# Pair 14 attended row by row, one-column scale and bias, more warm-up matmuls, and a re-sorted instruction order in an attention and gating kernel

## The chip, the cores and the metric

The kernel runs on one core of a Trainium2 chip, as one program with one launch. The metric is device time in microseconds (us), the median of several runs. The profile is one further execution of the same program, with its own time.

## The reference

Clustered attention comes first. Queries and keys are each assigned to the nearest of 16 centroids of their head. A query sees only the keys of its own cluster. Then a gated MLP mixes the tokens.

```
q_assign = argmax(q_n @ c_n^T);  k_assign = argmax(k_n @ c_n^T)      # (4, 8, 768), 16 clusters
scores   = where(q_assign == k_assign, q @ k^T / 8, -1e9)            # (4, 8, 768, 768)
attn     = exp(scores - max) / (sum + 1e-9);  x = attn @ v           # x: (4, 768, 512)
h = relu(x @ w_in);  u, v = split(h)                                 # w_in: 512 x 1024
v_s = w_spatial @ layernorm(v) + b_spatial;  out = (u * v_s) @ w_out # w_spatial: 768 x 768
```

## The kernel before

Four batches with eight heads each are worked as 16 pairs of heads, numbered 0 to 15, four to a batch. Pair n is prepared (prep), its shift is found (shifts), and it is attended (attend). After the four pairs of batch b, its MLP follows (mlp): six tiles each of V, U, S and O work. All products are taken in float16 parts, high and low, so most matmuls come in twos or threes.

There are two ways to attend a head. In the usual way, a first pass of matmuls (shifts, L1011) computes the scores of a head only for their row maxima, which VectorE reduces (L1018). The negated maxima go as three extra columns through a transposing DMA (sht<-shx, L1060) and a small DMA (hq<-sht, L1061) into the operands. The second pass (L1179, L1181) then has keys as rows, ScalarE takes exp with constant scale and bias (L1186), casts the result to its high part (L1201), GpSimd subtracts for the low part (L1202), and the value matmuls follow (L1208). A mean of the values enters for queries without keys, by small matmuls (L776, and L1208 from mean) and two DMAs.

In the other way (turned, for the heads listed in TURNED: both heads of pairs 11, 13 and 15) the scores are computed once, with queries as rows (L1086, L1088), two row tiles at a time. VectorE reduces the maxima (L1096, L1105) and makes a scale sl (L1106) and a bias bi (L1107) of two columns each, one column per row tile. ScalarE takes exp with them (L1115) and casts (L1125), GpSimd subtracts (L1126), and a transposing DMA of 128 x 1536 float16 per row tile (L1127, from one of three buffers to one of three others, named pt or wraw) brings the probabilities into the form that the value matmuls (L1134 to L1136) take.

Everything is first put down as operations with their dependences, and then a planner (Plan.run) issues them in the order of a simulated time. Among the operations that are ready on an engine it takes the one with the smallest due number. These numbers stand in a packed table (STARTS), one for each operation. Each engine runs its own list in that fixed order, and waits where an operand is not there. The planner's costs (DMA, LATE_PAD, PE_PAD and others) shape this order and nothing else. The eight PSUM banks are eight tiles named acc. A first group of matmuls of constants (keep_warm, L644) holds one of them from its first matmul to its last. These matmuls stand behind everything else in priority, and WARM lists the earliest planned time of each: 50, at 2.0 to 16.7 us. Five more stand ahead of the last O tile. SP's queue issues nearly all DMAs, in order, and ScalarE's queue the output.

Of the kernel before, what the change touches and what calls it, by code (L numbers as in the profile page):

```python
# [17 lines left out]
P = 128  # L18
# [51 lines left out]
LATE_PAD = 0.8  # L70
PE_PAD = 0.15
DMA = {
    "raw": (3.12, 0.57, 1.01, 0.36),
    "raw0": (1.26, 0.64, 1.0, 0.44),
    "vraw": (1.46, 0.43, 0.82, 0.36),
    "hqhq": (2.23, 0.77, 0.43, 0.68),
    "half": (0.25, 0.34, 0.88, 0.5),
    "lo": (0.95, 0.18, 1.02, 0.52),
    "mean": (0.0, 0.53, 0.43, 0.62),
    "row": (0.45, 0.7, 1.11, 0.61),  # L80
    "sht": (0.0, 0.51, 0.65, 0.73),
    "ohx": (1.39, 0.37, 0.53, 1.25),
    "shx": (0.9, 1.12, 0.53, 1.25),
    "xhl": (1.58, 1.01, 0.74, 1.4),
    "pt": (1.58, 1.01, 0.74, 1.4),
    "ghl": (1.55, 0.53, 0.67, 1.25),
    "out": (0.96, 0.07, 0.32, 0.34),
    "win": (1.77, 1.35, 0.88, 0.6),
    "wou": (1.12, 1.38, 0.9, 0.6),
    "wsp": (0.92, 0.17, 0.77, 0.55),  # L90
# [99 lines left out]
    "knv<9nL=ifg=9{dR~D7|WK~&LR+p`0Cpk~9mV4wOd0Nhp>*P*(RGyRf<VX2el8Ud=sVu6Ls;=s)daAx^rrM}Ns<P^-7O0b|f$F73s@ZC}+Nyr4OuC`2rK{_fx|8m&hw4#!w4S0T>IOPOPt*JKVSQbFP#g47eL|np"  # L190
    "H}qT0OqfY-Qkm?gj45s^nEa-&DP_{>uKJX&ZyK34rnd<<gUvki&^$G9>`1#wAJd7<Ff-XqF{{mPbHp^Xk#?e8XgAm=I>_8Lugp91*`%`L?G!uNZnAsqVVeqam_nwlnPV23WoCzYXTREDNCO$57*vDNW~^CfHkk|N"
    "qOmp;WQ5|-6k0<ESniIR)8>wGHm*%#Prx;J3U8pN>+80<W_}spF7NOM{1N}imx@_3R2-9uM0$}+lobO+FVRQL5og6Uaao)Zzh#heN~+8%wW^@XshBdMOe|B$Br>_oB-6-rGONribI5|Sk}NLE$U3r`oG;hPm2#2X"
    "CZEe%vbL-t8_CA9oopjJ%FeR4>?ViGVRDchDaXsPa<UZ4D^#H>r>d!n$?~$CtSqa@da{A6FZ;?4GD1#}O=Jt%P<EG1Wqa9E4wR8{rko_V$ksAS_LHMz4>?B8k;~+HIah9$C*^DTOumvz1=KjXSWcB|<TSZZu9v&y"
    "Q+Yt1kniPwc|`7(m*qiuTwahDC0Cc^U71*2mAB<X`9(gEPvjf<QYKK}B~$5DQB_QpRaI4O6;oFdRn%}XS&R`=M1NUA?H7a9IdMfi7GDIHz2smyTrQQH<VLwcwpIhx1$9H+Rd3WQ^;{j6XXP1rMc$B)<Slt!ev;qh"
    "2l+=nmM`Ql8AHWWAu5yVq&ll^YJi%q{z;>fs|+fY%A?|_FqK2)Qw3CEl|~g&rB!oPO*K_R)h%^X-B$ON(r@Kg`B_>8Dp+ZiQZ-g-RaVtq#Z`$^LX|=#RT))YRYUbw*;GL_Naa$+Rc_TtWmgqdOVvS5RDD%{HC3%r"
    "$J9AhLf6q<R7cfbjZke>A2m#kS1Z&QHAQVxqtrMxTFq0_)GReaEmgbK617&HQghWJwNPzT%hYPMR~=O^)E;$6y;bdWd)-0L(yR0#eM@A}D3i+QGOoNSzpDZ=w=OAb%9gT^94)WOJMx{3u41ZaDwZm(`)JUwRVw{M"
    "<<y0BE!9pnR6W!XH9<wFu_{sxS98>QHA$^hGu0ZkT^(0m$I&Tt8l6qI((BYFwMCs!m(>|{N!?S2)iw1@S*^9xOh?x-bTr*X&(#a{Y`s=r(7V(TwND*TJJo6RM7>w2FRH65uD+sPs)y>cdZa!oq5r5b{Z|F)jQWd`"
    "`nL+zTpJy%W9xD{sZOb@>P32^-l?DI=Q^Mh=;S)Jj-_+x%({^7tc&XkI$USb1$9wfNmtPobz|L3Pu6X8Z#`94)-`lJT~pW9t#uDQP%qIV^(4Js2OBU+%r~9Uj4`d$Rg+(pQI%8+l}Fb$O;k?PRrOPg)n>IpomXeo"
    "9ra6nQ=imVb;H~?C(Lnk(ws5Z%yo0c#M23Ne4SVq(D`*fol6(dC3P8HRyWs8bbZ}cx6nQHS#6Cop(d%xW4h^Hx~cB2`|1&ToSv^E^>`hn=jrKso1Uqc>eYIW_GXe9Z=%cuGvD;n!}TCNSP#%+^a{OPpVwRUUj0DN"
    "(9851eME28+x0<xT>sNo^=17<AJEtINqtLS*LU?({YI1dsDJ5%rnD(yN|@<pmU*S`>xcS-exzUPzgn2ICd9-t1<hw2*L>HpO>`6Aq%j#xK9kv`Fm=pVoy>5P#TZk?G%&?XN7K~QFg?s7v&1YgTg-N|-<&m<%mee)"  # L200
    "aC_6-GSAHy^Iy)`zlPb&Hml8Iv)TN%q^)4f+G;kB&1Xy5Wp=f#ZR^;kcCB4yx7p=(tKDID+P!v*Jz}re7xuUPY|q&n_My!JS>e6aAR!-=fa*{mnm{{f2rXa)jD?xd8-~CX_+|fD1B+oN><8t*g}ThHwQu7)_&q)^"
# [12 lines left out]
    "-4*x9-EuG7YxmBPfA7AyARmIUFgm8d<oLurbI;v3_tJfEpWQE)$^UiEXZK&-Z^ymy-<|crK87#iWBRzhtXJOq=swhk_(VRN&*{ti{JxNH>9b*O%!j401lGs<@Yg>B>D~glYVN9!=^pwlF0D)Na=N@OpDW;sxW=xk"
    "tL&P(7?=zh0xEPE4dY^b%;4TZHuoKJxo=R{rFH{dDL2ejax+~+H^+5!<6H+9+b8u&e3<X#pZG~`nw#ZjxQTAITkKZ3b#9B><c_!l?w~v5F1r)%tV{04`zSxzON@<id^8`+$Mf-hLZ8N`^of0HpV7DQZGC6I)u;Cv"
# [243 lines left out]
def kernel(  # L459
# [130 lines left out]
    def idt():  # L590
        return scratch.t[:, 0, 2 * D:2 * D + P]
# [853 lines left out]
```

## Time and profile before

| what | us |
|---|---|
| median of three runs | 651.34 (649.42 to 653.78) |
| profiled execution, its own time | 650.55 |
| its span, first to last instruction | 648.7 |
| TensorE (PE) busy, VectorE (DVE) busy | 626.9, 421.4 |
| ScalarE (ACT) busy, GpSimd (POOL) busy | 462.4, 443.3 |

A busy PE is not PE at its peak, since matmuls overlap and their ends are modelled. PEclk is the granted clock of TensorE: 1.00 is 2.4 GHz and 0.50 is 1.2 GHz. An idle engine matters only where the work that it delays ends last.

### The profile page before, as it was taken

The page shows a single profiled execution, that of the slowest core. Times are in us where ns is not written, and L with a number is a line of the kernel's source. Part 1 is how long each engine was busy: PE and PEld are TensorE (multiplying, and loading weights), DVE is VectorE, ACT ScalarE, POOL GpSimd, SP SyncE. Part 2 cuts the span into 40 slices and gives each one's busy share as a digit, 9 for nine tenths or more (in the row PEclk, how much of TensorE's full clock was granted, in tenths as well). Part 3 has the DMA queues.
Part 4 walks back from the last instruction along what each step waited for, and adds up shares of the span by engine and source line. Part 5 has one row for each costly group of instructions (what it writes and reads, how often), then busy time and mean ns, then how long its engine had stood idle before and what let it go on. Part 6 is the DMA issues. An engine that isn't in the chain of part 4 may idle for free.

```text
span 648.7 us, 16743 instructions
## 1 busy us (share of the span) xinstructions
PE 626.9 (97%) x6696; PEld 379.0 (58%) x6696; DVE 421.4 (65%) x795; ACT 462.4 (71%) x881; POOL 443.3 (68%) x376
## 2 busy tenths in 40 slices
PE   8889999999999999999999989999899999999997
PEld 3456777766676665466665645665556555444443
DVE  5969999999998996649667786754730961132000
ACT  5778899999999996268875878685778774242221
POOL 3476789899999997069984864786689775152210
PEclk9888999999999999999999999999899999999999
DMA  6575797979737588414636197964784479512223
GB/s 191 147 143 125 160 209 135 194 168 171 187 81 171 101 175 201 104 63 116 146 98 138 32 183 147 182 120 80 155 155 73 91 148 187 90 33 50 49 65 97
DMA packets 157975, 83.67 MB, mean 129 GB/s; under 512 B 142113, under 2 KB 145226, under 8 KB 157898
## 3 DMA queue, kind: packets, MB, share of 16 engines
q1 hardware_dynamic: 154154, 75.92, 58.4%
q10 hardware_dynamic: 3744, 6.69, 3.0%
q8 instruction: 52, 0.85, 0.6%
q14 instruction: 25, 0.20, 0.1%
HBM read 27.66 MB, written 6.29 MB: 52 GB/s over the span
## 4 chain that ended last, share of the span: by engine, by line
PE 68%; ACT 11%; DVE 9%; DMA 4%; issue 4%; POOL 4%; POOLq 0%; SPq 0%; ACTq 0%; DVEq 0%
PE acc L1280 33%; PE acc L1208 10%; PE acc L1181 6%; PE acc L1179 6%; PE acc L1011 5%; ACT p L1186 3%; ACT p L1115 2%; DVE nm L1018 2%; PE acc L644 2%; DVE nm L1096 2%; ACT pt L1201 2%; POOL pt L1202 2%; DMA gT<-ghl 1%; DMA sht<-shx 1%; DMA hq<-sht 1%
## 5 line engine op out<-in xcount | busy, mean ns | idle before, releaser
L1202 POOL TENSOR_TENSOR pt<-p,pt 128x768 f16<-128x768 f32 x148 | 252.0, 1723 | 35.6 <-ACT pt L1201 24.9
L1018 DVE TENSOR_REDUCE nm<-acc 128x1 f32<-128x512 f32 (+1 forms) x234 | 150.3, 680 | 24.2 <-PE acc L1011 21.4
L1186 ACT ACTIVATE p<-acc 128x512 f32<-128x512 f32 x234 | 129.0, 604 | 21.7 <-PE acc L1181 14.1
L1280 PE MATMUL acc<-win,xT 128*128 128x512 f16 x576 | 133.7, 379 | 0.2 <-ACT p L1115 0.2
L1201 ACT CAST pt<-p 128x768 f16<-128x768 f32 x148 | 120.2, 844 | 13.7 <-PE acc L1208 7.4
L1208 PEld LDWEIGHTS <-pt 128*128 128x128 f16 x2664 | 96.5, 97 | 20.2 <-POOL pt L1202 3.2
L1208 PE MATMUL acc<-vhl,pt 128*128 128x65 f16 x2664 | 103.5, 193 | 2.2 <-POOL pt L1202 2.1
L1280 PE MATMUL acc<-vn,wsp 128*128 128x512 f16 x432 | 101.4, 379 | 0.3 <-ACT p L1115 0.3
L1181 PE MATMUL acc<-hq 81*128 81x512 f16 (+1 forms) x312 | 91.7, 335 | 2.9 <-DMA hq<-sht 2.1
L1179 PE MATMUL acc<-hq,lo 128*128 128x512 f16 (+1 forms) x312 | 91.2, 333 | 0.4 <-ACT p L1186 0.2
L1280 PEld LDWEIGHTS <-xT 128*128 128x128 f16 x576 | 54.7, 98 | 60.6 <-issue 0.5
L1011 PE MATMUL acc<-hq 80*128 80x256 f16 (+1 forms) x312 | 78.6, 331 | 1.4 <-ACT p L1186 0.5
L1126 POOL TENSOR_TENSOR pt<-p,pt 128x768 f16<-128x768 f32 x36 | 59.0, 1644 | 26.1 <-ACT pt L1125 19.5
L1352 POOL TENSOR_TENSOR ghl<-u,ghl 128x512 f16<-128x512 f32 x24 | 28.5, 1189 | 64.8 <-ACT ghl L1351 64.8
L1280 PE MATMUL acc<-wou,gT 128*128 128x512 f16 x288 | 67.6, 379 | 0.6 <-DMA gT<-ghl 0.6
L1280 PEld LDWEIGHTS <-wsp 128*128 128x128 f16 x432 | 41.1, 98 | 45.6 <-issue 0.4
L1350 DVE SCALAR_TENSOR_TENSOR u<-acc,bsp,u 128x512 f32<-128x512 f32 x24 | 18.0, 748 | 75.6 <-PE acc L1280 73.6
L1115 ACT ACTIVATE p<-acc,bi,sl 128x512 f32<-128x512 f32 (+1 forms) x72 | 42.9, 676 | 14.2 <-DVE bi L1107 12.3
L1280 PEld LDWEIGHTS <-gT 128*128 128x128 f16 x288 | 27.5, 98 | 32.2 <-DMA gT<-ghl 1.3
L1179 PEld LDWEIGHTS <-lo 128*128 128x128 f16 x312 | 30.0, 99 | 26.8 <-issue 5.5
L1096 DVE TENSOR_REDUCE nm<-acc 128x1 f32<-128x512 f32 (+1 forms) x54 | 34.8, 680 | 11.2 <-PE acc L1088 11.1
L1011 PEld LDWEIGHTS <-hq 80*128 80x128 f16 x312 | 28.4, 100 | 20.0 <-issue 4.2
(154 smaller groups left out, 989.4 us busy)
## 6 DMA issues: line engine op xcount, KB each, us to landing
raw<-in_kqT_dram SPq DMA_DIRECT2D x15, 768.0 KB
vraw<-in_vp_dram SPq DMA_DIRECT2D x16, 384.0 KB
out_dram<-o ACTq DMA_DIRECT2D x24, 256.0 KB
hq<-hq SPq DMA_DIRECT2D x15, 384.0 KB
vn<-in_w_in_dram SPq DMA_DIRECT2D x8, 512.0 KB
hq<-lo SPq DMA_DIRECT2D x15, 192.0 KB
lo<-hq SPq DMA_DIRECT2D x15, 192.0 KB
wraw<-in_wsT_dram SPq DMA_DIRECT2D x12, 192.0 KB
```

What stands on the lines that cost most here:

```text
L1011: T.matmul(out=acc.t[:, c:c + cs.stop - cs.start], lhsT=hq.t[0:R_SH, 1, h, t * P:(t + 1) * P], rhs=hq.t[0:R_SH, 0, h, cs], start=c == 0, s ...
L1018: V.tensor_reduce(out=nm.t[:, t, k:k + 1] if n == 1 else nm.t[:, t:t + n, k], in_=src, axis=AX.X, op=ALU.max, negate=True)
L1096: V.tensor_reduce(out=nm.t[:, t, k:k + 1] if n_ == 1 else nm.t[:, t:t + n_, k], in_=src, axis=AX.X, op=ALU.max, negate=True)
L1115: A.activation(out=p32.t[:, j, halves[x]], in_=sc.t[:, j * (S - 512):(j + 1) * (S - 512)] if x else sc.t, func=AF.Exp, bias=bi.t[:, t:t + ...
L1126: c = op("POOL", 1.64, lambda pt=pt, j=j, p32=p32: G_.tensor_tensor(out=pt.t[:, S:], in0=p32.t[:, j, :], in1=pt.t[:, 0:S], op=ALU.subtract ...
L1179: T.matmul(out=o, lhsT=lo.t[:, h, ks], rhs=hq.t[:, 2, h, cs], start=x == 0, stop=False, skip_group_check=True)
L1181: T.matmul(out=o, lhsT=hq.t[0:R_E, 0, h, ks], rhs=hq.t[0:R_E, 1, h, cs], start=False, stop=True, skip_group_check=True)
L1186: o = op("ACT", 0.6, lambda: A.activation(out=p32.t[:, j0:j0 + n_, cs], in_=sc.t.rearrange("p (t c) -> p t c", t=n_), func=AF.Exp, bias=P_ ...
L1201: o = op("DVE" if fast else "ACT", C_CAST if fast else 0.83, lambda pt=pt, p32t=p32t, fast=fast: (V.tensor_copy if fast else A.copy)(out=p ...
L1202: o = op("POOL", 1.64, lambda pt=pt, p32t=p32t: G_.tensor_tensor(out=pt.t[:, S:], in0=p32t(), in1=pt.t[:, 0:S], op=ALU.subtract), after=[o ...
L1208: T.matmul(out=a[:, c * W:c * W + w], lhsT=lhsT, rhs=rhs, skip_group_check=True, **f)
L1280: T.matmul(out=acc.t[:, 0:w], lhsT=lr[m][0], rhs=lr[m][1], start=(m == 0), stop=(m == n - 1))
```

## The change

Both heads of pair 14 join TURNED. For the pairs in TS1 (11, 13 and 14) scale and bias are made one column at a time: four small operations for two row tiles in place of two, the bias by a tensor_scalar with the scale as its second operand, and each exp waits only for its own column. Pair 15 keeps the two-column form. WARM grows from 50 to 145 matmuls, the last at 45.2 us. The planner's DMA costs and pads change, it now reckons with instruction fetches that block the DMA rings (FETCH), and the table STARTS is another one, so the order on every engine is sorted anew.

```diff
-LATE_PAD = 0.8
-PE_PAD = 0.15
+LATE_PAD = 0.4
+FETCH = (128, 256, 2.6, 0.95)
+PE_PAD = 0.1
...
-    "pt": (1.58, 1.01, 0.74, 1.4),
+    "pt": (1.85, 1.01, 0.25, 1.42),
...
-TURNED = ((11, 0), (11, 1), (13, 0), (13, 1), (15, 0), (15, 1))
+TURNED = ((11, 0), (11, 1), (13, 0), (13, 1), (14, 0), (14, 1), (15, 0), (15, 1))
+TS1 = (11, 13, 14)
...
+                    count += 2 * o.mms
+                    while count >= nxt:
+                        fetch.append(s + FETCH[2])
+                        nxt += FETCH[1]
...
+            if n in TS1:
+                ys = []
+                for t in range(t0, t0 + 2):
+                    y = op("DVE", 0.1, lambda t=t: V.tensor_scalar(out=sl.t[:, t:t + 1], in0=nl.t[:, t:t + 1], scalar1=LIM, scalar2=SC_UNIT, op0=ALU.is_lt, op1=ALU.mult), after=[o], ...)
+                    ys.append(op("DVE", 0.1, lambda t=t: V.tensor_scalar(out=bi.t[:, t:t + 1], in0=nl.t[:, t:t + 1], scalar1=P_LOG * LN2 / SC_UNIT, scalar2=sl.t[:, t:t + 1], op0=ALU.add, op1=ALU.mult), after=[y], ...))
+            else:
+                (the two operations of before, with both columns)
+                ys = [o, o]
...
-                    e = op("ACT", (0.6, 0.4)[x], ex, after=[o], ...)
+                    e = op("ACT", (0.6, 0.4)[x], ex, after=[ys[j]], ...)
```

## Rows read from the trace of the kernel before

**Rows 1.** Busy time of each engine (instructions), then PEclk, DMA share, GB/s, by stretch
```profile
80.00:100.00 20.00, 19.63 (x291) 15.07 (x288) 18.71 (x35) 19.88 (x41) 17.91 (x13) 1.00 1.00 210
180.00:200.00 20.00, 20.00 (x317) 14.30 (x314) 19.12 (x33) 19.97 (x41) 19.76 (x15) 1.00 0.52 128
```
**Rows 2.** The chain that ended last: start us, us, what
```profile
553.87 75.12 PE acc L1280 x348
```
**Rows 3.** Columns as in the first group: stretches with a lowered clock
```profile
30.00:35.00 5.00, 5.00 (x50) 2.81 (x49) 2.48 (x6) 5.00 (x13) 4.61 (x3) 0.51 0.66 150
45.00:50.00 5.00, 4.00 (x13) 1.87 (x13) 1.57 (x3) 2.32 (x6) 2.13 (x2) 0.52 0.54 133
50.00:55.00 5.00, 5.00 (x62) 3.23 (x61) 4.31 (x7) 4.20 (x9) 3.28 (x3) 0.80 1.04 228
...
460.00:465.00 5.00, 4.40 (x45) 3.00 (x45) 4.46 (x11) 5.00 (x9) 2.64 (x2) 0.66 0.43 82
```
**Rows 4.** The chain that ended last, around 46 us: start us, us, what
```profile
42.99 2.97 DMA hq<-sht
...
48.72 0.43 PE acc L1179
```
**Rows 5.** Columns as in the first group: the room for them
```profile
20.00:40.00 20.00, 17.18 (x204) 10.86 (x202) 17.01 (x34) 14.68 (x37) 10.85 (x8) 0.83 0.68 166
40.00:60.00 20.00, 17.35 (x203) 11.64 (x203) 15.45 (x30) 13.41 (x25) 14.00 (x10) 0.83 0.59 123
```
**Rows 6.** VectorE in order of time: start us, us, instruction
```profile
5.66 0.15 DVE L620 TENSOR_SCALAR ninv<-nrm 128x1 f32<-128x1 f32 x1 [0.67 <-POOL nrm L618]
...
457.68 1.49 DVE L1107 SCALAR_TENSOR_TENSOR bi<-nl,sl 128x2 f32<-128x2 f32 x1
...
511.85 1.56 DVE L1106 TENSOR_SCALAR sl<-nl 128x2 f32<-128x2 f32 x1
...
517.28 0.17 DVE L1106 TENSOR_SCALAR sl<-nl 128x2 f32<-128x2 f32 x1
```
**Rows 7.** GpSimd in order of time, the same stretches
```profile
457.51 1.64 POOL L1126 TENSOR_TENSOR pt<-p,pt 128x768 f16<-128x768 f32 x1
...
511.74 3.24 POOL L1126 TENSOR_TENSOR pt<-p,pt 128x768 f16<-128x768 f32 x2 [0.18 <-ACT pt L1125]
```
**Rows 8.** Costliest groups: busy us, mean ns of one, then idle before
```profile
L1107 DVE SCALAR_TENSOR_TENSOR bi<-nl,sl 128x2 f32<-128x2 f32 x18 | 12.1, 671 | 0.4
```
**Rows 9.** TensorE in order of time: start us, us, instruction, idle before and its releaser
```profile
460.03 0.38 PE L1086 MATMUL acc<-lo,hq 128*128 128x512 f16 x1 [1.28 <-ACT p L1115]
```
**Rows 10.** Groups of instructions by form: the pass for maxima and the mean, 13 pairs
```profile
L1011 PE MATMUL acc<-hq 80*128 80x512 f16 x156 | 55.8, 384 | 1.0 <-DVE nm L1018 0.4 <-DVE hq L860 0.2 <-ACT p L1186 0.2
L1011 PE MATMUL acc<-hq 80*128 80x256 f16 x156 | 30.7, 279 | 0.4 <-ACT p L1186 0.3
...
L1208 PE MATMUL acc<-mean,hq 83*128 83x65 f16 x156 | 9.0, 193 | 1.1 <-DMA hq<-sht 1.1
```
**Rows 11.** Columns as in the first group: pairs 13, 14 and 15 in turn
```profile
440.00:480.00 40.00, 38.15 (x349) 21.59 (x347) 21.31 (x51) 27.75 (x48) 28.82 (x34) 0.96 0.71 136
480.00:505.00 25.00, 24.14 (x297) 15.21 (x296) 4.18 (x12) 21.71 (x40) 22.34 (x16) 1.00 0.49 88
505.00:550.00 45.00, 42.70 (x455) 24.66 (x454) 25.60 (x45) 29.85 (x49) 30.89 (x22) 1.00 0.78 139
```
**Rows 12.** DMA from 464 to 495 us: queue, packets, MB, share of 16 engines; then issues
```profile
q1 hardware_dynamic: 14664, 3.67, 73.9%
...
pt<-pt SPq DMA_TRANSPOSE x5
wraw<-pt SPq DMA_TRANSPOSE x3
gT<-ghl SPq DMA_TRANSPOSE x2
```
**Rows 13.** The chain that ended last, in pair 14: start us, us, what
```profile
486.88 5.44 DMA pt<-pt
```

More of the change, by code (lines that the diff above doesn't have):

```diff
@@ L284 @@
 class Op:
-    __slots__ = ("eng", "cost", "fn", "after", "order", "new", "claim", "key", "at", "dma", "turn", "cols", "due", "left", "ready", "outs", "end", "seq", "alt", "s", "free", "port", "tag", "gen", "post", "issue")
+    __slots__ = ("eng", "cost", "fn", "after", "order", "new", "claim", "key", "at", "dma", "turn", "cols", "due", "left", "ready", "outs", "end", "seq", "alt", "s", "free", "port", "tag", "gen", "post", "issue", "mms")
 LAG = {"PE": 0.2, "ACT": 0.034, "DVE": 0.034, "POOL": 0.034, "SP": 0.0, "NONE": 0.0}
@@ L317, in ring, with op @@
         return r
-    def op(self, eng, cost, fn, after=(), use=(), new=(), claim=(), key=0.0, at=0.0, dma=None, turn=False, cols=0, alt=None, due=None, port=None):
+    def op(self, eng, cost, fn, after=(), use=(), new=(), claim=(), key=0.0, at=0.0, dma=None, turn=False, cols=0, alt=None, due=None, port=None, mms=0):
         o = Op()
+        o.mms = mms
         o.due = self.due if due is None else due
@@ L361, in run @@
         hw = [0.0, FIRST]
+        count, nxt, fetch = 0, FETCH[0], []
         lanes = []
@@ L443, in run @@
                 hw[0] = h + o.gen
-                d = max(h + o.gen + 0.65, hw[1])
-                hw[1] = d + o.dma
-                o.end = d + o.dma + o.post
+                more = 0.0
+                while True:
+                    d = max(h + o.gen + 0.65, hw[1])
+                    x = d + o.dma + more
+                    if not fetch or fetch[0] >= x:
+                        break
+                    f = fetch.pop(0)
+                    if f > d:
+                        more += FETCH[3]
+                    else:
+                        hw[1] = max(hw[1], f) + FETCH[3]
+                hw[1] = x
+                o.end = x + o.post
                 lanes.append(o.end)
-                free[e] = max(s + o.issue, d + o.dma - 0.9 if o.turn else h)
+                free[e] = max(s + o.issue, x - o.turn if o.turn else h)
             o.s, o.free = s, free[e]
@@ L627 @@
     ct = r_acc.new()
-    o = op("PE", 0.3, lambda: T.transpose(out=ct.t[:, 0:P], in_=scratch.t[:, 0, 0:2 * D], identity=idt()), after=[o, ld_i], use=[scratch], new=[ct], key=KC)
+    o = op("PE", 0.3, lambda: T.transpose(out=ct.t[:, 0:P], in_=scratch.t[:, 0, 0:2 * D], identity=idt()), after=[o, ld_i], use=[scratch], new=[ct], key=KC, mms=1)
     c_cm = []
@@ L644, in run @@
                 T.matmul(out=tok.t, lhsT=ones, rhs=ones.unsqueeze(1).broadcast_to([P, 4, P]), start=True, stop=True)
-            o = op("PE", 0.2145, run, after=after, at=at, use=[tok] if k else [], new=[] if k else [tok], cols=512, key=FILLER + k)
+            o = op("PE", 0.2145, run, after=after, at=at, use=[tok] if k else [], new=[] if k else [tok], cols=512, key=FILLER + k, mms=1)
     if WARM:
@@ L1011, in scores @@
                         T.matmul(out=acc.t[:, c:c + cs.stop - cs.start], lhsT=hq.t[0:R_SH, 1, h, t * P:(t + 1) * P], rhs=hq.t[0:R_SH, 0, h, cs], start=c == 0, stop=c > 0 or n == 1, skip_group_check=True)
[L1013 removed]
+                o = op("PE", 0.2185, scores, after=ready(parts) + maxed[-MX_AHEAD:][:1], use=[hq], new=[acc], cols=512, key=K0_MX + K0_HEAD * h if n_ == 0 else K_MX, mms=n)
                 def most():
@@ L1088, in scores @@
                                 T.matmul(out=o, lhsT=hq.t[0:R_SH, 1, h, ts], rhs=hq.t[0:R_SH, 0, h, cs], start=False, stop=True, skip_group_check=True)
-                o = last["sc"] = op("PE", 0.436, scores, after=X["go"][h] + [last.get("sc")] + exps[-SQ_AHEAD:][:1], use=[hq, lo], new=[sc], cols=1024, key=K_SC)
+                o = last["sc"] = op("PE", 0.436, scores, after=X["go"][h] + [last.get("sc")] + exps[-SQ_AHEAD:][:1], use=[hq, lo], new=[sc], cols=1024, key=K_SC, mms=2 * len(spans))
                 new = not tops and t0 == 0
@@ L1117, in turned @@
                     new = not got and j == 0
-                    e = op("ACT", (0.6, 0.4)[x], ex, after=[o], use=[sc, sl, bi] + ([] if new else [p32]), new=[p32] if new else [], key=K_EXP)
+                    e = op("ACT", (0.6, 0.4)[x], ex, after=[ys[j]], use=[sc, sl, bi] + ([] if new else [p32]), new=[p32] if new else [], key=K_EXP)
                     exps.append(e)
@@ L1136, in values @@
                         T.matmul(out=o, lhsT=l, rhs=vh.t[:, k, h, 0:D + 1], start=False, stop=k == NT - 1, skip_group_check=True)
-                prev = op("PE", 0.545, values, after=[c, prev] + X["v"] + (xread.get(b - 2, []) if t == 0 else []), use=[tp, vh] + ([av] if t else []), new=[] if t else [av], cols=18 * 65, key=AV_KEY)
+                prev = op("PE", 0.545, values, after=[c, prev] + X["v"] + (xread.get(b - 2, []) if t == 0 else []), use=[tp, vh] + ([av] if t else []), new=[] if t else [av], cols=18 * 65, key=AV_KEY, mms=3 * NT)
                 plan.tag = "s%d%d" % (n, 2 * h + t0 // 3)
@@ L1181, in scores @@
                                     T.matmul(out=o, lhsT=hq.t[0:R_E, 0, h, ks], rhs=hq.t[0:R_E, 1, h, cs], start=False, stop=True, skip_group_check=True)
-                    o = last["sc"] = op("PE", 0.436, scores, after=X["go"][h] + [X["shift"][h][0 if len(X["shift"][h]) == 1 else spans[0][1].start // 512], last.get("sc")] + exps[-SC_AHEAD:][:1], use=[hq, lo], new=[sc], cols=1024, key=K_SC)
+                    o = last["sc"] = op("PE", 0.436, scores, after=X["go"][h] + [X["shift"][h][0 if len(X["shift"][h]) == 1 else spans[0][1].start // 512], last.get("sc")] + exps[-SC_AHEAD:][:1], use=[hq, lo], new=[sc], cols=1024, key=K_SC, mms=2 * len(spans))
                     j0, cs = spans[0][0] % 2, spans[0][1]
@@ L1226, in attend @@
                 plan.tag = "a%d%d" % (n, 2 * h + k // 3)
-                prev = op("PE", (C_F32 if whole else 0.516 if two else 0.545) + (0.175 if k == 0 else 0), values, after=got + [prev] + X["v"] + (xread.get(b - 2, []) if k == 0 else []), use=[pt, X["vf"] if whole else vh, mw] + (avs if k else [hq]), new=[] if k else avs, cols=18 * 65, key=AV_KEY)
+                prev = op("PE", (C_F32 if whole else 0.516 if two else 0.545) + (0.175 if k == 0 else 0), values, after=got + [prev] + X["v"] + (xread.get(b - 2, []) if k == 0 else []), use=[pt, X["vf"] if whole else vh, mw] + (avs if k else [hq]), new=[] if k else avs, cols=18 * 65, key=AV_KEY, mms=NT * ((1 if whole else 2 if two else 3) + (k == 0)))
                 if whole:
```

153 lines of the change are left out of this document (78 added, 75 removed).

## The prediction

> **What bounds the kernel now.** I read the busy time of each engine in stretches of 20 us first, because the stages have different limits. Up to 140 us only attention runs, and ScalarE and VectorE are full: 19.88 and 18.71 of 20 us [rows 1]. From about 180 us the MLP of an earlier batch fills every gap of TensorE, which is busy 20.00 of 20 [rows 1], and the end is TensorE alone: 348 MLP matmuls in 75.12 us, 0.216 us each [rows 2]. So the time is TensorE's work plus the time in which it stands or runs at half clock, wherever that is. Two places have such time. The first is 20 to 60 us, where TensorE is busy 17.18 and 17.35 of 20 us at a mean clock of 0.83 [rows 5]. The second is the last batch of attention, 440 to 550 us: 38.15 of 40, 24.14 of 25 and 42.70 of 45 us busy, 5.0 us idle in all [rows 11]. An early microsecond saved is saved at the end too, since what follows is bound by full engines first and by TensorE's list of work later.
>
> **Matmuls of constants.** The granted clock is 0.51 in 30 to 35 us, 0.52 in 45 to 50 and 0.80 in 50 to 55 [rows 3]; it is the lower level, 1.2 GHz, most of that time. It falls after TensorE stood waiting for a DMA that lands at 42.99 + 2.97 = 45.96 us [rows 4]. A step of 512 columns then takes 0.43 us [rows 4], twice the 0.216 of a full-speed one [rows 2]. From 46.0 to about 51.5 us the chain that ended last runs through these slow steps, with VectorE busy 1.57 and ScalarE 2.32 of 5 us [rows 3]: nothing else is full. At full clock 5.5 us become 2.75, so constants in the wait before 46 us give 2.7 us. At 30 to 35 us ScalarE is busy all 5.00 us [rows 3]: there the slow steps lie beside full work, which hides the gain. I take 0 there, with 3 as the other end.
>
> The cost: 95 more matmuls at 0.216 us are 20.5 us of TensorE. Between 20 and 60 us there are 2 x 20 - 17.18 - 17.35 = 5.5 us idle [rows 5] and about 5.7 us that the full clock would free (half of about 11.5 slow us), room for 11.2 / 0.216 = 52. The planner sets the others into whatever gaps it sees later, and 80 to 100 us has only 0.4 idle [rows 1]. Those 43 stand in TensorE's list ahead of real work, and one that is met at a bad moment delays it by up to 0.216 us. TensorE isn't full there, so I take 0.5 us, with 0 and half of all (43 x 0.108 = 4.6 us) as ends. Also, the group holds one PSUM bank of eight from its first matmul to its last, so longer than now. Term: -2.7 + 0.5 = **-2.2**.
>
> **One column at a time.** At 511.85 us the two-column scale takes 1.56 us [rows 6]. The first of GpSimd's two subtractions runs from 511.74 for half of 3.24 us [rows 7], so both end at 513.4. Later the same scale takes 0.17 us [rows 6]. So the two-column form waits for a running subtraction, and 18 biases take 671 ns on the mean [rows 8]. No row shows a one-column tensor_scalar beside a subtraction. The nearest is 0.15 us in the preamble [rows 6], with no subtraction running; the other end is a wait as long as now, so no gain and two more operations a group. I take 0.15, the nearer in form.
>
> What it is worth is read at TensorE, not at VectorE. In pair 13 a bias of 1.49 us [rows 6], behind a subtraction from 457.51 [rows 7], ends at 459.17. Exp follows, and TensorE has stood 1.28 us by then [rows 9]; after it the clock is 0.66 for 5 us [rows 3], which is 3.4 us at half clock and costs 1.7. With the bias 1.3 us earlier the stand mostly goes, and perhaps half of the slow time. That is -1.3 - 0.9 = **-2.2**, ends -3.0 and +0.5 (the added operations, 0.33 us a group, stay beside TensorE's work; VectorE is busy 21.31 of 40 [rows 11]). Pair 15 keeps its waits.
>
> **Pair 14 turned.** TensorE loses one pass: 12 matmuls of 512 columns and 12 of 256, a thirteenth of those in [rows 10]. At 0.216 us and half of it that is 3.9 us. Twelve matmuls of the mean add 9.0 x 12 / 156 = 0.7 [rows 10], so 4.6 us, all of it in the last batch's list of work. The reductions are as many as before, so VectorE is even. ScalarE has 24 exps in place of 18 and no shift columns. It is busy 21.71 of 25 us in pair 14's stretch [rows 11], and the stretch can grow by MLP work, so I count nothing for it. Two shx transposes, two small DMAs behind them and two of the mean leave SP's queue. Twelve transposes of pt join it. Behind them wait the loads of pair 15, the transposes of gT and the xT of pairs 13 and 14.
>
> Turned pairs have more waiting. The stretches of pairs 13 and 15 hold 1.85 and 2.30 us idle, that of pair 14 only 0.86 [rows 11], and a row tile passes through exp, cast, subtraction and a transpose that took 5.44 us once [rows 13] before its values can start. The rows of pairs 13 and 15 let me expect 1.2 us more idle and as much again in slow clock or partly filled steps, 2.4 us. Net **-2.2**, ends -4.6 and +3.
>
> **The order.** The new table and the planner's costs move every instruction. No row prices that. What it could take out or add is of the size of the idle time left in the two places above, so I take 0, with ends of -4 and +4.
>
> The sum is -2.2 - 2.2 - 2.2 = -6.6 us. Against the profiled execution's 650.55 that is 643.9. The median of the runs lies 0.8 us above that execution, so I say **644.7**.
>
> **Rivals.** *The transposes fill the DMA engines.* From 464 to 495 us queue q1 is busy 73.9% of 31 us, 22.9 us, for eight transposes of pt and two of gT, which are two thirds as long [rows 12]: 22.9 / 9.33 = 2.45 us each. Twelve more are 29.4, less 2.5 for the two half as long that leave, so +27 us. From 440 to 550 us the engines are now busy 0.71 x 40 + 0.49 x 25 + 0.78 x 45 = 75.8 us [rows 11]. 103 of 110 us is nearly full, and then each transpose waits for the one before. TensorE's saved 4.6 us would be spent waiting, with some 2 us more: the pair's term is +2 and the time 644.7 + 4.2 = 649. For it speaks the share; against it that most of these waits are hidden by MLP work, and that the copies can move to emptier stretches. The Trainium skill (Advanced Engine Details and Errata, X-Bar Transpose) says that transposing DMAs are as fast as regular ones, at 350 to 400 GB/s; by that page one of 393 KB would take about 1.05 us, an estimate, and this rival would not come. The 3.67 MB in 22.9 us of the same row don't bear that out, so it lowers no chance here.
>
> *All that is counted comes, and no new wait.* The 3 us at 30 to 35 us come in part (1.5), and pair 14 keeps its 4.6: 644.7 - 1.5 - 2.4 is about 641.
>
> *Slower: the constants get in the way.* Their place is 60 to 140 us, where ScalarE and VectorE are full and TensorE feeds them through eight banks, one of them held, with a constant ahead of many a step. Four pairs have 4 x 36 = 144 groups of scores and maxima. Delayed by 0.1 us each, they cost 14 us, so 658.7. It decides when ScalarE's idle time in these 80 us grows by more than 7 us, which eats up the whole gain. Against it: the list places them only where the planner sees a gap, and TensorE has some idle time there.
>
> *It doesn't do what it says:* the one-column bias waits too (its scale is one more operand from SBUF). That takes 2.2 us away and gives 647, within the range. By the Trainium skill (SBUF — State Buffer, Who interferes with whom) VectorE waits for GpSimd with two SBUF inputs or in a two-port mode; it doesn't say whether a scale operand counts as an input.
>
> **How the numbers follow.** Forecast 0.45, transposes 0.25, all of it 0.16, slower 0.14. About 1% (6.5 us) is what a measurement of this kernel can tell from no change. Faster by over 1% means below 644.8: half of the forecast, nearly all of the 641 case and a little of the transposes, 0.43. Slower by over 1% means above 657.9: half of the slow case and a little more, 0.09. The rest, 0.48, is within. The range runs from 637, where the order's -4 is added to the 641 case, to 655, which leaves out most of the slow case: about 0.17 outside.
>
> **What would show it.** A clock of 1.00 in 45 to 55 us and a first pass of pair 1 done some 2.7 us sooner; one-column operations near 0.15 us beside subtractions; 288 matmuls of L1011's line, 24 fewer; TensorE's idle time in the last batch near 5 us; q1's share there under 0.9. The prediction is wrong if ScalarE has gaps in 60 to 140 us, or if the stand before the last MLP grows: it begins later than 547 us though less work is ahead of it.

## The result, and the profile after

The changed kernel takes **654.84 us** (median of 10 runs, 653.68 to 655.86), the kernel before 649.98 beside it. The ratio is 1.0078, with a 95% interval of 1.0061 to 1.0096: slower by 5 us, where 644.7 had been forecast with a range up to 655. The profiled execution took 654.75 us, its span is 652.9.

Stretches of the kernel after, columns as in [rows 1]; the last three answer to [rows 11], those in 45 to 55 us to [rows 3]:

```profile
45.00:50.00 5.00, 5.00 (x62) 3.30 (x61) 5.00 (x11) 4.75 (x11) 3.45 (x3) 1.00 0.76 205
50.00:55.00 5.00, 5.00 (x84) 4.16 (x82) 5.00 (x10) 4.41 (x10) 3.82 (x4) 1.00 0.73 134
60.00:140.00 80.00, 76.82 (x1059) 56.40 (x1057) 73.42 (x135) 68.90 (x139) 62.46 (x39) 1.00 0.72 164
440.00:480.00 40.00, 38.11 (x403) 22.08 (x403) 24.80 (x68) 31.13 (x52) 26.98 (x23) 1.00 0.92 152
480.00:505.00 25.00, 23.80 (x241) 13.64 (x240) 17.62 (x43) 20.74 (x36) 22.27 (x25) 1.00 0.99 174
505.00:550.00 45.00, 43.14 (x420) 23.59 (x419) 16.99 (x35) 26.49 (x44) 27.59 (x21) 1.00 0.85 153
```

The clock is full in 45 to 55 us, as forecast. The last batch is fuller of DMA (0.92, 0.99 and 0.85 for 0.71, 0.49 and 0.78), with TensorE 4.95 us idle for 5.0 before. These two places are as forecast or near it. The loss is in 60 to 140 us: ScalarE is busy 68.90 of 80 us. In the kernel before the same row is

```profile
60.00:140.00 80.00, 77.68 (x1163) 58.88 (x1162) 76.85 (x146) 76.65 (x157) 66.99 (x44) 1.00 0.83 168
```

so that ScalarE's idle time grew from 3.35 to 11.10 us, by 7.75. All four engines do less there, although TensorE also carries constants. What grew most is ScalarE's wait for a buffer of p in these 80 us (in all, times, longest), before and after:

```profile
ACT p L1186 <- POOL pt L1202: 0.9, 2, 0.5
...
ACT p L1211 <- POOL pt L1227: 5.8, 3, 3.0
```

The groups of the kernel after that answer to [rows 10], the constants, and the one- and two-column scale and bias (the last four from 360 to 560 us):

```profile
L1029 PE MATMUL acc<-hq 80*128 80x512 f16 x144 | 52.0, 379 | 1.7 <-DVE nm L1036 1.2 <-DVE hq L878 0.4
L1029 PE MATMUL acc<-hq 80*128 80x256 f16 x144 | 27.5, 271 | 0.1
L662 PE MATMUL acc<-ones 128*128 128x512 f16 x150 | 44.5, 398 | 1.6 <-DVE ones L621 1.6
L1128 DVE TENSOR_SCALAR bi<-nl,sl 128x1 f32<-128x1 f32 x36 | 5.9, 205 | 0.0
L1130 DVE TENSOR_SCALAR sl<-nl 128x2 f32<-128x2 f32 x6 | 4.9, 810 | 0.1
L1127 DVE TENSOR_SCALAR sl<-nl 128x1 f32<-128x1 f32 x36 | 3.7, 141 | 0.2
L1131 DVE SCALAR_TENSOR_TENSOR bi<-nl,sl 128x2 f32<-128x2 f32 x6 | 1.9, 312 | 0.1
```

The pass has 288 matmuls, 24 fewer, and one-column operations take 141 and 205 ns on the mean where pair 15's two-column scale still takes 810.

What a stand in 60 to 140 us looks like: ScalarE, GpSimd and TensorE in order of time, around 73 us.

```profile
70.28 1.56 ACT L1226 CAST pt<-p 128x768 f16<-128x768 f32 x2
74.84 1.09 ACT L1211 ACTIVATE p<-acc 128x512 f32<-128x512 f32 x2 [3.00 <-POOL pt L1227]
...
71.58 3.24 POOL L1227 TENSOR_TENSOR pt<-p,pt 128x768 f16<-128x768 f32 x2 [1.96 <-PE acc L1206]
78.05 3.24 POOL L1227 TENSOR_TENSOR pt<-p,pt 128x768 f16<-128x768 f32 x2 [3.23 <-issue]
...
75.49 0.38 PE L1204 MATMUL acc<-hq,lo 128*128 128x512 f16 x1 [1.10 <-ACT p L1211]
```

Behind two casts the next in ScalarE's list is an exp. It needs a buffer of p that GpSimd's two subtractions give back at 74.82, so ScalarE stands 3.00 us; then TensorE stands 1.10 for the exp's bank and GpSimd 3.23 for its next row tile. Three engines wait for each other in turn, each bound to its own fixed order. From 108 us on the chain that ended last runs for long stretches through VectorE:

```profile
108.58 0.68 DVE acc L717
109.26 2.34 DVE lo L912
111.60 0.60 DVE acc L718
112.21 0.59 DVE nm L1036
112.80 0.60 DVE acc L719
113.40 1.80 DVE nm L1036 x3
```

Pieces of weights (acc) and a lo of 2.34 us stand between the maxima (nm), and the chain waits for all of them. From 104 to 140 us nm makes 24.5% of the chain and lo 20.2%; before, TensorE's value matmuls lead it there with 34.1%. The changed kernel's chain meets the last long run of MLP matmuls at

```profile
547.78 94.55 PE acc L1305 x438
```

which answers to [rows 2] and begins 6 us earlier. The counts in the two lines do not compare, since the chain of before leaves TensorE at 629.02 us and comes back to it later. Counted in the trace, 462 matmuls of the MLP are left at 547.78 us, and 435 in the kernel before: 27 more, 5.8 us at 0.216.

### The profile page after: what moved, and what is told of

The parts are those of the page before. It is cut to its first block, busy times and chain, and to the rows that moved or that the text cites. A ratio compares the mean times of both kernels' runs of the same rounds, so it can differ in the third digit from the quotient of the medians.

```text
span 652.9 us, 16935 instructions
## 1 busy us (share of the span) xinstructions
PE 634.0 (97%) x6753; PEld 381.2 (58%) x6753; DVE 419.6 (64%) x845; ACT 467.8 (72%) x879; POOL 443.9 (68%) x376
## 4 chain that ended last, share of the span: by engine, by line
PE 54%; ACT 11%; DVE 10%; DMA 7%; issue 3%; POOL 3%; SPq 0%; POOLq 0%; ACTq 0%; DVEq 0%
PE acc L1305 31%; PE acc L1233 8%; ACT p L1140 4%; PE acc L1204 4%; PE acc L1206 4%; PE acc L1029 3%; DVE nm L1036 3%; DMA wraw<-pt 3%; ACT pt L1150 2%; POOL pt L1151 2%; DMA pt<-pt 1%; DVE nm L1114 1%; DVE lo L912 1%; ACT pt L1226 1%; ACT p L1211 1%
## 5 line engine op out<-in xcount | busy, mean ns | idle before, releaser
L1227 POOL TENSOR_TENSOR pt<-p,pt 128x768 f16<-128x768 f32 x136 | 227.5, 1694 | 43.9 <-ACT pt L1226 29.8
L1211 ACT ACTIVATE p<-acc 128x512 f32<-128x512 f32 x216 | 119.1, 603 | 23.1 <-PE acc L1206 11.7
L1226 ACT CAST pt<-p 128x768 f16<-128x768 f32 x136 | 110.0, 842 | 8.7 <-PE acc L1233 7.2
L1151 POOL TENSOR_TENSOR pt<-p,pt 128x768 f16<-128x768 f32 x48 | 80.3, 1688 | 31.2 <-ACT pt L1150 24.2
L1233 PEld LDWEIGHTS <-pt 128*128 128x128 f16 x2448 | 86.8, 97 | 12.5 <-POOL pt L1227 0.3
L1233 PE MATMUL acc<-vhl,pt 128*128 128x65 f16 x2448 | 92.1, 193 | 0.2 <-POOL pt L1227 0.2
L1204 PE MATMUL acc<-hq,lo 128*128 128x512 f16 (+1 forms) x288 | 82.0, 325 | 2.1 <-ACT p L1211 1.3
L1206 PE MATMUL acc<-hq 81*128 81x512 f16 (+1 forms) x288 | 82.2, 326 | 0.0
L1029 PE MATMUL acc<-hq 80*128 80x256 f16 (+1 forms) x288 | 72.0, 325 | 1.8 <-DVE nm L1036 1.2
L1140 ACT ACTIVATE p<-acc,bi,sl 128x512 f32<-128x512 f32 (+1 forms) x96 | 57.7, 676 | 15.5 <-DVE bi L1131 5.9
L1150 ACT CAST pt<-p 128x768 f16<-128x768 f32 x48 | 39.8, 843 | 10.5 <-DMA pt<-pt 5.4
L662 PE MATMUL acc<-ones 128*128 128x512 f16 x150 | 44.5, 398 | 1.6 <-DVE ones L621 1.6
```

The source lines that it names most:

```text
L1029: T.matmul(out=acc.t[:, c:c + cs.stop - cs.start], lhsT=hq.t[0:R_SH, 1, h, t * P:(t + 1) * P], rhs=hq.t[0:R_SH, 0, h, cs], start=c == 0, s ...
L1140: A.activation(out=p32.t[:, j, halves[x]], in_=sc.t[:, j * (S - 512):(j + 1) * (S - 512)] if x else sc.t, func=AF.Exp, bias=bi.t[:, t:t + ...
L1151: c = op("POOL", 1.64, lambda pt=pt, j=j, p32=p32: G_.tensor_tensor(out=pt.t[:, S:], in0=p32.t[:, j, :], in1=pt.t[:, 0:S], op=ALU.subtract ...
L1204: T.matmul(out=o, lhsT=lo.t[:, h, ks], rhs=hq.t[:, 2, h, cs], start=x == 0, stop=False, skip_group_check=True)
L1206: T.matmul(out=o, lhsT=hq.t[0:R_E, 0, h, ks], rhs=hq.t[0:R_E, 1, h, cs], start=False, stop=True, skip_group_check=True)
L1211: o = op("ACT", 0.6, lambda: A.activation(out=p32.t[:, j0:j0 + n_, cs], in_=sc.t.rearrange("p (t c) -> p t c", t=n_), func=AF.Exp, bias=P_ ...
```

## The experiments

Each has its own time of the kernel before beside it, so they are compared by ratios; 0.001 is 0.65 us.

**Are the constants in the way?** Theory 1 said yes, the rival said that the order itself is at fault. Two runs keep the order and the banks of the changed kernel and only don't issue the later constants.

```diff
-            if o.fn is not None:
+            if o.fn is not None and not FILLER + 50 <= o.key < FILLER + 145:      # in the first run
+            if o.fn is not None and not FILLER + 95 <= o.key < FILLER + 145:      # in the second
                 o.fn()
```

> The changed kernel with the same order on every engine and the same banks, but the constants 51 to 145 are not issued (the bank that they would hold stays empty). Theory 1, constants get in the way: TensorE is the bound in 60 to 220 us too, so the 50 constants that ran after 60 us come back at 0.216 us each, 10.8 us, and the wait before 46 us loses its clock again (2.7 us): 654.8 - 10.8 + 2.7, about 647, ScalarE's idle time in 60 to 140 us back near 3 us. Rival, the new order itself (VectorE's lo operations and exps wait for GpSimd's subtractions): TensorE's gaps only get wider, 654 to 657.

> The changed kernel, same order and same banks, constants 96 to 145 not issued, which are those that ran after 60 us. Theory 1: 654.8 - 50 x 0.216 = 644, clock 1.00 in 45 to 55 us. Rival (the order): within 2 us of 654.8.

Measured: 650.72 us, ratio 1.0021 (1.0000 to 1.0041), and 652.03 us, 1.0037 (1.0024 to 1.0050), where the changed kernel has 1.0078. So the 50 constants behind 60 us cost 2.7 us, 0.05 each and not 0.216. The 45 between them and the first 50 cost about 1 us more than the clock gives, which the intervals don't separate from nothing. Neither theory's number came. The stretch of the run without constants settles where the rest is:

```profile
60.00:140.00 80.00, 72.64 (x1025) 53.58 (x1021) 73.59 (x135) 68.27 (x136) 60.90 (x39) 1.00 0.69 164
```

ScalarE is busy 68.27 us, no more than with the constants. Its gaps belong to the order (which was planned with all 145 constants in it).

The same 95 constants planned anew (WARM cut to 95, the due numbers kept), so that the bank is free from about 60 us:

> The changed kernel with 95 constants, planned anew from the same due numbers, so that the bank is free from about 60 us on and the order may differ. Theory that the held bank costs: some 5 us less than the run in which the 50 last constants are only left out. Theory that the matmuls themselves cost: the same as that run, 644. Rival (the order with its due numbers): 652 or more.

Measured: 655.51 us, 1.0074 (1.0049 to 1.0098), as the rival said. A freed bank gave nothing that shows, and a new order from the same due numbers took 2.4 us more than the old one without those constants, by intervals that touch.

To see what a constant costs where it is truly in the way, 67 went ahead of steps in the kernel before:

```diff
+            if e == "PE" and o.new and o.cols in (512, 1024) and 60 <= s < 150 and o.key < FILLER:
+                self.seen = getattr(self, "seen", 0) + 1
+                if self.seen % 2 == 0:
+                    self.constant(o.new[0])        # 512 columns, into the step's own bank
```

> The kernel before, same order and banks, with one more matmul of constants ahead of every second one of the 134 steps of scores and of the maxima pass between 60 and 150 us, 67 in all, into the bank that the step itself fills next (so no bank is held). Theory 1: 67 x 0.216 = 14.5 us if TensorE is the bound there, so 664; at least 7 us. Rival: ScalarE and VectorE are the bound there and TensorE has room, 650 to 652.

Measured: 661.77 us, 1.0192 (1.0157 to 1.0227): 12.5 us, 0.19 for each constant of 0.216. So TensorE's list has next to no room there in the order of before, and ScalarE falls behind too when something is put ahead of its steps (70.01 of 80 us busy). The planner's later constants cost about a quarter of that each; they stand in gaps of its plan.

**The clock in 45 to 55 us, alone.** The kernel before with 20 constants in its waits, 10 of them ahead of the step that waits to 46 us:

```diff
+            for _ in range({266: 4, 280: 4, 377: 2, 412: 10}.get(o.seq, 0)):
+                self.constant(o.new[0])
```

> The kernel before, same order and banks, with 20 more matmuls of constants in the waits before 47 us alone: 4, 4 and 2 ahead of three steps between 24 and 28 us, 10 ahead of the step that waits for a DMA at 43 to 46 us, each into the bank that its step fills next. If the clock term is right: clock 1.00 in 45 to 55 us and 647 (2.7 us less). Rival, the constants delay as much as the clock gives: 649 to 650.

Measured: 650.35 us, 1.0026 (0.9990 to 1.0063): no gain. In the profiled execution the clock is 1.00 in 40 to 60 us, but not all executions are alike: five of ten have a mean clock of 0.997 and take 647.4 to 649.5 us, the other five 0.986 to 0.992 and 651.2 to 654.6. The two runs that follow begin with the same instructions as the kernel before and have no such constants. In their executions, first stretches 45 to 55 us and then TensorE's step behind the wait, pairs 11 and 13 in one-column form:

```profile
45.00:50.00 5.00, 4.94 (x62) 3.42 (x62) 4.22 (x8) 4.46 (x11) 2.70 (x2) 1.00 0.76 172
50.00:55.00 5.00, 4.93 (x82) 3.86 (x79) 5.00 (x11) 4.53 (x9) 5.00 (x5) 1.00 0.97 206
...
45.06 0.38 PE L1187 MATMUL acc<-hq 81*128 81x512 f16 x1 [1.28 <-DMA hq<-sht]
```

and the order of before up to 300 us:

```profile
45.00:50.00 5.00, 3.99 (x56) 2.78 (x56) 3.42 (x7) 3.78 (x10) 3.26 (x3) 1.00 0.55 134
50.00:55.00 5.00, 4.94 (x81) 3.60 (x79) 5.00 (x11) 4.53 (x9) 5.00 (x4) 1.00 1.00 227
...
46.01 0.38 PE L1196 MATMUL acc<-hq 81*128 81x512 f16 x1 [2.09 <-DMA hq<-sht]
```

TensorE stands 1.28 and 2.09 us and keeps the upper level. Others that begin with the same instructions do not keep it: 45 to 50 us of the run with 67 constants, the first of which begins at 65.75 us, and of the one that puts pair 14's pass back, further down.

```profile
45.00:50.00 5.00, 2.91 (x10) 1.47 (x10) 1.01 (x3) 1.97 (x5) 2.51 (x2) 0.70 0.50 122
...
45.00:50.00 5.00, 5.00 (x34) 2.81 (x32) 3.90 (x9) 0.91 (x4) 1.00 (x1) 0.57 0.70 152
```

Of ten profiled executions with these first instructions, that of before among them, four have a lowered clock in 45 to 50 us (0.52, 0.56, 0.57 and 0.70) and six have 1.00. The 0.52 of [rows 3] comes and goes from one execution to the next. It goes with the time: of 71 executions of the kernel before, 29 have a mean clock up to 0.989 and a median of 650.6 us, and 25 have 0.994 or more and a median of 647.9, 2.7 us less.

**One column at a time, alone.** The kernel before, its order and due numbers, with TS1:

```diff
+TS1 = (11, 13)
```

> The kernel before with one part of the change alone: scale and bias one column at a time in pairs 11 and 13 (due numbers of before, pair 14 not turned, 50 constants). Theory that the one-column form doesn't wait for GpSimd: the small operations take about 0.1 to 0.2 us beside subtractions, TensorE's stand of 1.28 us in pair 13 goes, 649.6 - 2.2 = 647.4. Rival, one-column operations wait as well or the wait is only replaced by the next one: 649 to 650.

Measured: 645.94 us, 0.9946 (0.9916 to 0.9976): 3.5 us less. The theory's number holds. VectorE and GpSimd of the changed kernel show why, around 468 us and in pair 15, which keeps two columns:

```profile
468.16 0.21 DVE L1127 TENSOR_SCALAR sl<-nl 128x1 f32<-128x1 f32 x2
469.14 0.32 DVE L1128 TENSOR_SCALAR bi<-nl,sl 128x1 f32<-128x1 f32 x2
521.75 1.41 DVE L1130 TENSOR_SCALAR sl<-nl 128x2 f32<-128x2 f32 x1
...
466.15 3.24 POOL L1151 TENSOR_TENSOR pt<-p,pt 128x768 f16<-128x768 f32 x2 [0.88 <-ACT pt L1150]
...
519.89 3.25 POOL L1151 TENSOR_TENSOR pt<-p,pt 128x768 f16<-128x768 f32 x2
```

From 466.15 to 469.39 a subtraction runs; two scales take 0.21 us together and two biases 0.32. The two-column scale at 521.75 begins inside subtractions that end at 523.14 and lasts to 523.16. But the stand for which the term was counted did not go. In the run with the one-column form alone TensorE and its clock show

```profile
460.10 1.46 PE L1286 MATMUL acc<-win,xT 128*128 128x512 f16 x6 [1.47 <-ACT p L1121]
...
460.00:465.00 5.00, 4.90 (x39) 2.54 (x39) 1.17 (x4) 5.00 (x11) 4.59 (x4) 1.00 0.75 143
```

a stand of 1.47 us, and a full clock behind it where [rows 3] has 0.66. TensorE's idle time in 440 to 550 us is the same, 5.01 us before and 5.04 here. Where the 3.5 us lie is not shown by this. Some of them may be the clock of other stretches: executions with a mean clock of 0.994 or more have a median of 645.6 us in this run and of 647.7 in the kernel before beside it, 2.1 us apart.

**Is it the order up to 220 us?** The order of before is forced up to 300 us; then the due numbers of the changed kernel hold, with pair 14 turned, TS1 = (11, 13, 14), 50 constants and the planner's costs of before.

```diff
+            forced = [o for q in wait.values() for o in q if o.due is not None and o.due < 0]
+            if forced or done < 1974:      # the first 1974 operations in the order of before
+                o = min((o for o in forced if gate(o) is not None), key=lambda o: o.due)
```

> The order of the kernel before up to 300 us, then pair 14 turned and one column at a time, with the due numbers of the changed kernel for the rest; 50 constants as before. Theory 2, the new order up to 220 us is what costs: this run keeps TensorE's progress of before at 220 us and gets what pair 14 and the one-column form bring later, 643 to 646. Rival, the turned pair 14 fills the DMA engines and the last batch loses what it saved: 650 to 653.

Measured: 639.14 us, 0.9844 (0.9787 to 0.9902); once more 641.52 us, 0.9884 (0.9857 to 0.9910). That is some 8 to 10 us faster than before and 13 to 15 faster than the changed kernel.

> The version with the order of before up to 300 us, pair 14 turned and one column at a time, once more with five rounds: 639 to 640, ratio 0.985 to the kernel before.

The 20 constants of above on top of it:

> The run with the order of before up to 300 us and the two later parts, and the 20 constants in the waits before 47 us. If both theories hold the gains add up: 641 to 644. If the clock's gain is taken up by a fuller stretch behind it, or the last batch is bound by its transposes, the same as without the constants.

Measured: 640.42 us, 0.9875 (0.9809 to 0.9942). They add nothing that shows here either.

The closest pair is made to differ in the first 300 us alone; the rest of each is planned from the same due numbers with the new costs. One starts with the order of before, the other with that of the changed kernel (constants from the 51st on left out):

> The order of before up to 300 us, then pair 14 turned and one column at a time with the due numbers of the changed kernel, the rest planned with the changed kernel's own costs (instruction fetches, smaller pads); 50 constants. Theory 2, what costs is the order up to 220 us and not the planner's costs for the last batch: 639 to 643, as with the old costs (639.1). Rival, the new costs make the last batch's order bad: 647 or more.

> The other half of the pair: the order of the changed kernel up to 300 us (without the constants from the 51st on), then the same due numbers and the same planner costs as in the run beside it. Theory 2: the 10 to 11 us that TensorE is behind at 220 us stay to the end, so 10 us more than the run beside it, 649 to 653. Rival, the stretch up to 220 us only moves work that is got back later: within 3 us of the run beside it.

Measured: 643.70 us, 0.9933 (0.9910 to 0.9956), and 656.31 us, 1.0126 (1.0094 to 1.0158). The one that starts with the changed kernel's order takes **12.6 us** more. The stretch from 60 to 140 us, and ScalarE's waits for a buffer of p from 60 to 220 us (in all, times, longest), with the order of before:

```profile
60.00:140.00 80.00, 77.28 (x1153) 58.43 (x1152) 76.24 (x146) 76.09 (x155) 69.09 (x45) 1.00 0.80 168
...
ACT p L1217 <- POOL pt L1233: 2.5, 3, 1.7
```

and with that of the changed kernel:

```profile
60.00:140.00 80.00, 74.37 (x1037) 54.68 (x1035) 73.25 (x139) 70.74 (x144) 64.64 (x40) 1.00 0.74 174
...
ACT p L1217 <- POOL pt L1233: 7.8, 4, 3.0
```

Every engine does 3 to 5 us less in the second, with no constants behind the 50th. Work of TensorE that is done by 220 us, estimated by pricing each 20 us group of matmuls in proportion at 0.216 us for 512 columns [rows 2], is some 7.5 us less; by 300 us it is 7 us less. The other 5 us and more are lost behind 300 us, where the planner goes on from two different states. 440 to 560 us, with the order of before first:

```profile
440.00:560.00 120.00, 115.05 (x1056) 62.72 (x1055) 51.07 (x130) 72.07 (x119) 73.64 (x67) 1.00 0.80 147
...
440.00:560.00 120.00, 111.55 (x1078) 62.56 (x1077) 58.01 (x144) 77.54 (x129) 77.06 (x69) 0.97 0.84 150
```

In the second TensorE is busy 3.5 us less and its clock is lower. The late list alone can do as much: the changed kernel without its constants from the 51st on has the same order up to 300 us and takes 1.0021, 6.8 us less than this run's 1.0126. Beside the fastest version (0.9844 and 0.9884), which has the early order of before and another late list, that run of 1.0021 is 9 to 11.5 us slower. So the early order costs about 7 us by the work that is missing at 300 us, and up to 12.6 with what follows from it.

Do the planner's new costs make that order, or the new due numbers? The operations and due numbers of before, planned with the new costs (FETCH, pads and landing times as in the diff of the change):

> The operations and due numbers of the kernel before, planned with the changed kernel's costs (instruction fetches, other landing times, smaller pads); 50 constants. If the new costs make the bad order: 655 to 660, with TensorE some 10 us behind at 220 us. If it is the due numbers that make it: 648 to 652, and TensorE's progress at 220 us within 3 us of before.

Measured: 652.44 us, 1.0050 (1.0031 to 1.0069), 3.3 us slower. By the same estimate TensorE is 4.6 us behind before at 220 us. So the costs alone bring a part of the loss. The other part comes with the due numbers or with the 95 further constants that the planner had to place; these were not separated.

**Pair 14.** Pair 14 turned inside the due numbers and costs of before, its new operations at places carried over from the changed kernel's list:

> Due numbers and planner costs of the kernel before throughout, pair 14 turned (its new operations at places carried over from the changed kernel's list), one column at a time in 11, 13 and 14. If pair 14's gain doesn't need the new order of the last batch: 639 to 642. If it does: 645 or more, no better than the one-column form alone (645.9).

Measured: 648.78 us, 0.9992 (0.9972 to 1.0012). That is 3 us more than the one-column form alone (0.9946), by intervals that touch: turned in the old list, at places that were made for another, pair 14 loses. Whether pair 14 or its places lose there is not shown. In the new list for the last batch the same operations give 0.9844 and 0.9884. Then the saved pass was put back there as work:

```diff
+            if o.seq in PASS:                  # 12 of the 18 score steps of pair 14
+                self.constant(o.new[0], 512)
+                self.constant(o.new[0], 256)
```

> The version of 639.1 us with the pass that pair 14 no longer makes put back as work: 12 matmuls of constants of 512 columns and 12 of 256 ahead of 12 of its 18 score steps, into the steps' own banks, 3.9 us at the full clock. If that work was on the path that sets the end: 643. Rival, in the last batch TensorE waits for transposes anyway: 639 to 640.

Measured: 642.18 us, 0.9883 (0.9855 to 0.9911), beside 641.52 and 0.9884 without it: 0.7 us for 3.9 us of work by the medians and nothing by the ratios, which the intervals don't tell from 0; the rival's case. And the new list without pair 14 turned:

> The order of before up to 300 us, then the due numbers of the changed kernel and one column at a time in pairs 11 and 13, but pair 14 not turned. Theory that turning pair 14 saves its pass of TensorE work (4.6 us) and costs little in waits: 4 to 6 us more than the run with pair 14 turned (639.1), so 643 to 646. Rival, the gain comes from the new order of the last batch and not from pair 14: 639 to 641.

Measured: 663.18 us, 1.0233 (1.0201 to 1.0264), which neither theory expected. TensorE is busy only 14.96 and 16.01 us in 420 to 440 and 440 to 460:

```profile
420.00:440.00 20.00, 14.96 (x96) 6.12 (x92) 15.13 (x27) 3.75 (x10) 4.66 (x4) 0.79 0.33 71
440.00:460.00 20.00, 16.01 (x100) 7.67 (x99) 11.40 (x39) 12.97 (x23) 9.32 (x11) 0.87 0.48 71
```

The places carried over for pair 14's pass and shift were bad ones, so this run says nothing of pair 14. Last, the one-column form in pair 15 too (TS1 = (11, 13, 14, 15)):

> As the run of 639.1 us (order of before up to 300 us, pair 14 turned, one column at a time in 11, 13 and 14), and scale and bias one column at a time in pair 15 too. If pair 15's two-column waits end on the path they go: 637.5. If TensorE's MLP work hides them, or the added operations delay as much: 639 to 640.

Measured: 640.96 us, 0.9876 (0.9850 to 0.9902): no gain beside 0.9844 and 0.9884. Either pair 15's two-column waits are hidden or the added operations cost as much; this run does not tell which.

## Why the prediction was wrong

**The order** is the step that failed: "No row prices that ... so I take 0, with ends of -4 and +4." It was the largest term of all. Its part up to 300 us costs 7 to 12.6 us; its part behind that gains: with the order of before and pair 14 at carried-over places the same operations take 0.9992, with the new due numbers behind 300 us 0.9844 to 0.9884, 7 to 10 us less. Both lie beyond the bounds. The bounds were taken from the idle time left in two places, which limits what an order can take out, but not what it can add: a list that was full can be made to wait anywhere. The term looked at the two idle places only. In 60 to 140 us ScalarE and VectorE were full, and that was a place with much to lose; in the prediction it stands only in the rival on constants. That the measured 654.84 lies within the range up to 655 is luck: no end of the range was worked out from such a loss.

**Matmuls of constants**, taken as -2.2, cost about 3.7 (1.0078 less 1.0021). The cost half was mis-sized: 0.5 us was taken, 2.7 measured for those behind 60 us, inside the end of 4.6. The gain half, -2.7, took one execution for all: the row with a clock of 0.52 is true, but six of ten executions have 1.00 there. As the difference between executions with a high and a low mean clock its size came out (647.9 and 650.6 us), but the median of before holds only part of it. The 20 constants of the run of 1.0026 did not hold the clock in half of its executions, so it doesn't settle what a held clock gives. The mean clock of the 71 executions of before lies between 0.984 and 1.00, and the profiled one had 0.987, near the low end. What the 145 constants do bring is an even clock: 0.999 or 1.00 in all ten runs of the changed kernel, with times within 2.2 us.

**One column at a time**, -2.2, measured -3.5 with pairs 11 and 13 alone: the number held. The durations (0.15 us taken, 141 and 205 ns on the mean) hold too. The way to the time does not: TensorE still stands 1.47 us in pair 13.

**Pair 14 turned**, -2.2, depends on the list. The 4.6 us of work are gone (288 matmuls), but they are worth 0.7 of 3.9 where they were put back, since other waits set the pace in that batch. More waiting was taken at 2.4; in the old list, at the places given, what is lost is more than what is saved. The last batch of the changed kernel shows the forecast's idle time of 5 us (4.95).

**The rivals.** *Slower: the constants get in the way* had the right side, place and sign to watch: ScalarE's idle time grew by 7.75 us, beyond its point of 7. But its cause fell. With the constants taken out the gaps stay (11.73 us idle), so the sign was right and its culprit wrong. The other sign, a last run of MLP matmuls that begins later than 547 us, came as 547.78. *The transposes fill the DMA engines* came as a share, 0.92 and 0.99 in the changed kernel and 0.97 and 0.91 in the fastest version, without the price (q1's share in 464 to 495 us is 85.0%, under the 0.9 forecast): that version has TensorE busy 107.91 of 110 us there. *The one-column bias waits too* did not come.

From the runs the sum is -3.5 for one column, -4 to -7 for pair 14 together with the late list (0.9884 or 0.9844 less 0.9946), +7 to +12.6 for the early list and +3.7 for the constants: 0 to 9, where 5 was measured. The planner's costs for the last batch, 0.9933 against 0.9844 to 0.9884, would add to it; the terms come from different lists and do not add exactly.

## What to carry to other kernels

A new instruction order is a change of its own, and in a list this full the largest one: price it by forcing the old order for a stretch and the new one for the rest, not by the idle time that is left. Read the work that is done at the end of the stretch too, since what follows is planned anew and adds its own difference. When a change mixes a good part and a new order, measure the part inside the old order first; here half of the change was worth 8 to 10 us once the early order of before was kept. A slow clock in one profiled execution may be absent in the next: compare the mean clock and the time of many executions before pricing it.

## What the runs showed of the hardware that was not expected

A one-column tensor_scalar of VectorE (128x1, f32) runs beside GpSimd's subtraction in 0.10 to 0.17 us even with a second operand from SBUF, while the two-column form of the same operation with constants only waits to the subtraction's end (1.41 us at 521.75). The same first instructions met a clock of 0.52 to 0.70 in 45 to 50 us in four profiled executions and of 1.00 in six: 0.52 behind a stand of 2.14 us, 1.00 behind stands of 1.28 and 2.09 us. Executions of one kernel with a mean clock up to 0.989 and from 0.994 on differ by 2.7 us in their medians (650.6 and 647.9).
